# The second product of the last 768 tokens by seven block products in place of eight

## The chip, the cores and the metric

The kernel runs on one core of a Trainium2 chip. The metric is device microseconds of one execution, the median of several. PE is the engine that multiplies matrices, PEld its weight loads, DVE the vector engine, ACT the scalar engine, SP the queue from which all transfers (DMAs) of this kernel are issued.

## The reference, cut to what matters

Three stages follow each other on 4 x 576 = 2304 tokens of width 512: attention, a gated block (`_moe_ref`), and this block, the only one that the change touches:

```python
def _moe2_ref(x, g_ln, w_ch1, w_ch2) -> np.ndarray:    # x 2304 x 512, w_ch1 512 x 2048, w_ch2 2048 x 512
    mu = np.mean(x, axis=-1, keepdims=True)
    var = np.mean((x - mu) ** 2, axis=-1, keepdims=True)
    xn = (x - mu) / np.sqrt(var + 1e-06) * g_ln
    ch = np.maximum(xn @ w_ch1, 0.0) @ w_ch2
    return (x + ch).astype(np.float32)
```

Everything is float32. The kernel splits each operand into a high and a low part (`split`: ACT writes the high part, DVE the difference) and adds three matmuls for one product: low weight by high data, high by low, high by high.

## The kernel before

The last stage, `last_stage`, does `_moe2_ref` in three thirds of 768 tokens (`sc` = 0, 1, 2; `TC`, `TH` = 768, 384), each third in two halves of 384. Features lie on the 128 partitions, tokens along the row.

**First product.** The 2048 hidden features are 16 blocks of 128, worked in 8 pairs. `pair` does a pair for both halves at once: a 2 x 2 block product (2 halves by 2 feature blocks) by seven block products with sums of weights and of data (Strassen's scheme in Winograd's form) in place of eight. One `product` is 6 matmuls of 128x384, a pair 42. The combined weights `w1[i]` of a pair are made in the first third (`piece`, `combine`), written to HBM (`keep`) and read back in the other thirds (`fetch`, 1792 KB) into two buffers in turn: the fetch for pair i + 2 can start when pair i has done its last matmul. The sums of the seven products go through DVE: u2 = p6 + p1, u3 = p7 + u2, and so on (lines 839 to 865); p1 is copied by ACT (`s`, L840), since p2 is added onto it in its bank.

**Second product.** It is done straight (`ch2`): for a hidden block f, 4 output blocks of 128 features, 3 matmuls each, 12 in all. Half 0 runs among the pairs, two pairs' blocks behind; the hidden blocks of half 1 are kept unsplit (`late`) and half 1 follows after the pairs, each block split by `to_h` (L793 on ACT, L794 on DVE) three buffers ahead of PE. A third is 336 matmuls of the first product and 384 of the second. `leave` scales each output block by the row's factor, adds x and stores it (L826, L828, L829).

**Beside it.** `prepare` works through `units`: loading and converting the weights in the first third (DVE, ACT). `norm`, `expand` and `rsqrt` make the next third's normalised data, on DVE and ACT. The program is written in this order, but a planner, with costs of its own, sets the order on every engine: it may move an instruction ahead of one that it takes to be waiting. On the chip each engine then runs its own list in order, and a waiting instruction holds back all behind it; that goes for SP's list of transfers too.

## Time and profile before

| | us |
|---|---|
| median of 3 runs (lowest, highest) | 687.57 (685.63, 692.07) |
| the profiled execution | 686.18 |
| its span, first to last instruction | 684.4 |
| first matmul of the last stage's first product | 296.5 |
| last matmul of the kernel starts | 679.83 |

The profile page gives busy time and instructions of each engine, the chain that ended last, and groups of equal instructions with their mean time. A matmul's bar lasts some 335 ns while the next starts some 174 ns after it, since they are pipelined: PE's rate is to be read from starts, not from bars. The granted clock is full throughout (0.999 in the mean). The views used further on are shown as rows ahead of the prediction.

### The profile page before, as it was taken

How to read it: one execution, taken by the hardware profiler on the slowest of the kernel's cores; microseconds unless marked ns; L12 is line 12 of the kernel's file. 1: busy time of each engine (PE TensorE's matmuls, PEld its weight loads, DVE VectorE, ACT ScalarE, POOL GpSimd, SP SyncE). 2: the span in 40 equal slices, each digit the busy share in tenths (PEclk: the TensorE clock that was granted, in tenths of full speed). 3: DMA queues.
4: the chain of work that ended last, by engine and by line, in shares of the span. 5: the costliest groups of instructions: out<-in, count | busy, mean ns of one | idle time of the engine just before them, and what ended most of it. 6: DMA issues, size and time to landing. Idle time of an engine off the chain costs nothing.

```text
span 684.4 us, 12749 instructions
## 1 busy us (share of the span) xinstructions
PE 663.7 (97%) x5050; PEld 635.6 (93%) x5050; DVE 466.2 (68%) x990; ACT 318.9 (47%) x794; POOL 19.6 (3%) x24
## 2 busy tenths in 40 slices
PE   5899999999998999999999999999999999999997
PEld 4689979989897989989999999999999999999997
DVE  4989787586759686899989993733669355333523
ACT  3988966283458447644454952111365222111121
POOL 0011011000200011000000000000000000000000
PEclk9999999999999999999999999999999999999999
DMA  8873233457552550449796634534354425352001
GB/s 267 290 195 121 85 100 114 141 157 213 161 149 78 167 181 1 169 165 387 253 347 232 247 132 160 196 136 191 124 199 154 139 75 210 121 203 107 25 23 46
DMA packets 34987, 110.58 MB, mean 162 GB/s; under 512 B 3760, under 2 KB 14256, under 8 KB 31856
## 3 DMA queue, kind: packets, MB, share of 16 engines
q1 hardware_dynamic: 34928, 109.78, 47.1%
q8 instruction: 39, 0.64, 0.4%
q14 instruction: 20, 0.16, 0.1%
HBM read 83.02 MB, written 26.74 MB: 160 GB/s over the span
## 4 chain that ended last, share of the span: by engine, by line
PE 69%; DVE 10%; DMA 8%; ACT 8%; issue 2%; SPq 1%; POOL 1%; DVEq 0%; ACTq 0%; POOLq 0%
PE ps_p L788 24%; PE ps_o L204 10%; PE ps_o L205 10%; PE ps_o L203 9%; DMA w_scratch<-w_p 3%; ACT pt L400 2%; DMA qk<-in_qk_l 2%; PE ps_g L203 1%; PE ps_pv L458 1%; DMA y_scratch<-y 1%; PE ps_g L205 1%; DMA n<-y_scratch 1%; PE ps_g L204 1%; PE ps_t L439 1%; ACT pts L400 1%
## 5 line engine op out<-in xcount | busy, mean ns | idle before, releaser
L788 PE MATMUL ps_p<-x,w 128*128 128x384 f32 x1008 | 184.1, 335 | 1.3 <-DVE u L844 1.1
L788 PEld LDWEIGHTS ps_p<-x,w 128*128 128x128 f32 x1008 | 175.0, 188 | 3.0 <-DVE u L844 1.5
L205 PE MATMUL ps_o<-h,w 128*128 128x384 f32 x384 | 128.3, 334 | 0.0
L204 PE MATMUL ps_o<-h,w 128*128 128x384 f32 x384 | 128.3, 334 | 0.0
L203 PE MATMUL ps_o<-h,w 128*128 128x384 f32 x384 | 126.8, 334 | 0.1
L203 PEld LDWEIGHTS ps_o<-h,w 128*128 128x128 f32 x384 | 71.9, 188 | 0.4 <-ACT h L793 0.4
L204 PEld LDWEIGHTS ps_o<-h,w 128*128 128x128 f32 x384 | 72.1, 188 | 0.1
L205 PEld LDWEIGHTS ps_o<-h,w 128*128 128x128 f32 x384 | 72.1, 188 | 0.0
L794 DVE SCALAR_TENSOR_TENSOR h<-late,h 128x384 fp32r<-128x384 f32 x48 | 26.5, 556 | 41.6 <-ACT h L793 41.6
L793 ACT ACTIVATE h<-late 128x384 fp32r<-128x384 f32 x48 | 25.3, 526 | 63.4 <-PE ps_o L205 63.2
L840 ACT ACTIVATE s<-ps_p 128x384 f32<-128x384 f32 x24 | 11.8, 491 | 58.9 <-PE ps_p L788 56.1
L203 PE MATMUL ps_g<-wsg,vn 128*128 128x288 f32 x128 | 39.0, 304 | 0.0
L205 PE MATMUL ps_g<-wsg,vn 128*128 128x288 f32 x128 | 38.2, 299 | 0.0
L203 PE MATMUL ps_u<-xhl,winl 128*128 128x288 f32 x128 | 38.1, 297 | 0.0
L793 ACT ACTIVATE h<-c 128x384 fp32r<-128x384 f32 x24 | 12.6, 524 | 54.3 <-DVE c L857 54.2
L204 PE MATMUL ps_g<-wsg,vn 128*128 128x288 f32 x128 | 37.9, 296 | 0.0
L203 PE MATMUL ps_y<-gt,wout 128*128 128x288 f32 x128 | 37.8, 298 | 0.0
L204 PE MATMUL ps_u<-xhl,winh 128*128 128x288 f32 x128 | 37.8, 295 | 0.0
L205 PE MATMUL ps_u<-xhl,winh 128*128 128x288 f32 x128 | 37.7, 295 | 0.0
L205 PE MATMUL ps_y<-gt,wout 128*128 128x288 f32 x128 | 37.5, 295 | 0.0
L204 PE MATMUL ps_y<-gt,wout 128*128 128x288 f32 x128 | 37.5, 294 | 0.0
L203 PE MATMUL ps_v<-winh,xhl 128*128 128x512 f32 x80 | 31.9, 399 | 0.3 <-DVE xhl L495 0.2
(179 smaller groups left out, 1316.4 us busy)
## 6 DMA issues: line engine op xcount, KB each, us to landing
w<-w_scratch SPq DMA_DIRECT2D x16, 1792.0 KB, 7.5
w_scratch<-w SPq DMA_DIRECT2D x8, 1792.0 KB, 7.5
stg<-in_w_ch SPq DMA_DIRECT2D x22, 512.0 KB, 6.2
raw_p<-in_w_ch SPq DMA_DIRECT2D x20, 256.0 KB, 3.1
qk<-in_qk_s SPq DMA_DIRECT2D x8, 601.0 KB, 4.5
...
```

The costliest lines, as they stand in the source:

```text
L203: nc.tensor.matmul(ps, lhsT=ll, rhs=rh, start=first, stop=False)
L204: nc.tensor.matmul(ps, lhsT=lh, rhs=rl, start=False, stop=False)
L205: last_mm[0] = nc.tensor.matmul(ps, lhsT=lh, rhs=rh, start=False, stop=last)
L400: exps.append(nc.scalar.activation(p3[:, i, :], src, AF.Exp, scale=SCALE, bias=mx[:, i:i + 1], accum_out=sm[:, i:i + 1]))
L439: nc.tensor.transpose(ps[:rows, (t - t0) * c:(t - t0 + 1) * c], src, ident)
L458: nc.tensor.matmul(ps[64 * h:64 * h + 64, (i - b0) * QB:(i - b0 + 1) * QB], lhsT=vt[:LW, (i * 2 + h) * D:(i * 2 + h + 1) * D], rhs=pT[:LW, ...
L788: nc.tensor.matmul(o, lhsT=w[:, a, n0 + nk * k, :], rhs=x[:, c, k, :], start=first and k == 0 and n == 0, stop=k == 1 and n == 2, skip_gro ...
L793: nc.scalar.activation(h[:, 0, :], src, AF.Relu)
L794: nc.vector.scalar_tensor_tensor(out=h[:, 1, :], in0=src, scalar=0.0, in1=h[:, 0, :], op0=ALU.max, op1=ALU.subtract)
L840: nc.scalar.activation(s1, a, AF.Copy)
```

## The change

The second product of the last third is done by seven block products too, over 2 halves by 2 sets of output blocks, with the sum over the 8 pairs accumulated in PSUM. The last third so becomes two stretches: `last_pair` eight times (336 matmuls, no second product among them), and then seven products of 48 matmuls (336). The operands:

- The weights of the second product are combined too. `store2` writes each pair's converted weights to HBM in the first third (512 KB); `combine2` in the second third reads them back, makes four sums on DVE, splits 1792 columns (ACT, DVE) and stores high and low parts as 14 pieces of 128 columns a partition (runs of 512 bytes; a partition's 14 pieces lie 1 MiB apart in `w2_scratch`), 896 KB each. `fetch2` reads one slice of 1024 KB for each product and output set in the last third, into four buffers in turn.
- The hidden blocks stay in SBUF as sums (`hb`) and are split for the next product by `grain` while PE does the present one.
- `out2` adds up the products and stores the outputs.

In the other two thirds `pair` gets another order, in which p6, p5 and p3 are added onto p1's bank and p4 onto p7's (the sign of one data sum is turned for it). DVE makes two sums fewer a pair; ACT makes copies of the running sum (`u2`, `u4`) and one relu more. The steps of `norm` in the first third stand earlier.

```diff
+WX2 = {1: (0, 2, 0), 2: (4, 2, 2), 7: (1, 2, 1), 4: (5, 2, 2), 5: (8, 1, 0), 6: (10, 1, 1), 3: (12, 1, 3)}
+ORDER2 = (1, 2, 7, 6, 5, 4, 3)
+XTAGS = (0, 4, 1, 5, 2, 3, 6)
...
-NORM_AT = ({3: (0,), 4.5: (1,), 5: (2,), 5.5: (3,), 6: (4,), 6.5: (5,)}, {2: (0,), 3: (1,), 4: (2,), 5: (3,), 6: (4,), 6.5: (5,)})
+NORM_AT = ({1: (0,), 3: (1,), 3.5: (2,), 4.5: (3,), 5: (4,), 6: (5,)}, {2: (0,), 3: (1,), 4: (2,), 5: (3,), 6: (4,), 6.5: (5,)})
...
+    w2f_d = nc.dram_tensor("w2f_scratch", (NW, P, 2 * DM), F32, kind="Internal").ap()
+    w2_d = nc.dram_tensor("w2_scratch", (14, P, NW, 2, P), F32, kind="Internal").ap()
...
+    def store2(i):
+        nc.sync.dma_start(out=w2f_d[i], in_=big["stg"][:, 2048:3072].bitcast(F32))
+
+    def combine2(i):
+        stg = big["stg"]
+        c = stg[:, 0:1792].bitcast(F32)
+        wf = c[:, 0:1024].rearrange("p (k e r f) -> p k e r f", k=2, e=2, r=2)
+        nc.sync.dma_start(out=c[:, 0:1024], in_=w2f_d[i])
+        s = c[:, 1024:1792].rearrange("p (s e f) -> p s e f", s=3, e=2)
+        a11, a21, a12, a22 = wf[:, 0, :, 0], wf[:, 0, :, 1], wf[:, 1, :, 0], wf[:, 1, :, 1]
+        tt = nc.vector.tensor_tensor
+        tt(out=s[:, 0], in0=a21, in1=a22, op=ALU.add)
+        tt(out=s[:, 1], in0=s[:, 0], in1=a11, op=ALU.subtract)
+        tt(out=a21, in0=a11, in1=a21, op=ALU.subtract)
+        tt(out=s[:, 2], in0=a12, in1=s[:, 1], op=ALU.subtract)
+        hi, lo = stg[:, 1792:3584].bitcast(F32R), stg[:, 0:1792].bitcast(F32R)
+        split(hi, lo, c)
+        for h, src in enumerate((hi, lo)):
+            nc.sync.dma_start(out=w2_d[:, :, i, h, :].rearrange("n p f -> p n f"),
+                              in_=src.bitcast(F32).rearrange("p (n f) -> p n f", f=P))
+
+    w2s, slices = {}, {}
+    places = (("w2", 0), ("w2", NW - 1), ("w1", 0), ("w1", 1))
+
+    def fetch2(n):
+        m, e = ORDER2[n // 2], n % 2
+        n0, step, _ = WX2[m]
+        place = places[n % 4]
+        shape = [P, 2, 2, DM] if place[0] == "w2" else [P, 2, 14, P]
+        w = big[place].tile(shape, F32R, tag=place[0], name="w2c")
+        w = w.rearrange("p a b c -> p (a b c)")[:, :2 * NW * P]
+        nc.sync.dma_start(out=w.bitcast(F32), in_=w2_d[n0 + step * e].rearrange("p i h f -> p (i h f)"))
+        slices[m, e] = w.rearrange("p (i h f) -> p i h f", i=NW, h=2)
...
+        units += [(store2, (i,))]
...
-                tt(out=b21, in0=t2, in1=b21, op=ALU.subtract)
+                tt(out=b21, in0=b21, in1=t2, op=ALU.subtract)
...
-        b = bank(role, "ps_p6")[:, :TH]
-        product(sc, i, b, 6, True)
+        b = bank(role, "ps_p7")[:, :TH]
+        product(sc, i, b, 7, True)
+        product(sc, i, a, 6, False)
         u2 = tmp("u2")
-        tt(out=u2, in0=b, in1=s1, op=ALU.add)
-        product(sc, i, a, 2, False)
-        h1 = to_h(a)
-        d = bank(role, "ps_p7")[:, :TH]
-        product(sc, i, d, 7, True)
-        u3 = tmp("u3")
-        tt(out=u3, in0=d, in1=u2, op=ALU.add)
+        nc.scalar.activation(u2, a, AF.Copy)
+        c = bank(role, "ps_p2")[:, :TH]
+        product(sc, i, c, 2, True)
+        c11 = tmp("c11")
+        tt(out=c11, in0=c, in1=s1, op=ALU.add)
+        h1 = to_h(c11)
+        product(sc, i, a, 5, False)
+        u4 = tmp("u4")
+        nc.scalar.activation(u4, a, AF.Copy)
+        tt(out=late(f2), in0=b, in1=u4, op=ALU.add)
         if i:
             ch2(sc, 0, f1 - 2, 1 - role)
         mid()
-        e = bank(role, "ps_p4")[:, :TH]
-        product(sc, i, e, 4, True)
+        product(sc, i, a, 3, False)
+        nc.scalar.activation(late(f1), a, AF.Relu)
+        product(sc, i, b, 4, False)
         c21 = tmp("c21")
-        tt(out=c21, in0=u3, in1=e, op=ALU.subtract)
+        tt(out=c21, in0=b, in1=u2, op=ALU.add)
         h2 = to_h(c21)
-        c = bank(role, "ps_p5")[:, :TH]
-        product(sc, i, c, 5, True)
-        tt(out=late(f2), in0=c, in1=u3, op=ALU.add)
         if i:
             ch2(sc, 0, f2 - 2, 1 - role)
-        product(sc, i, c, 3, False)
-        tt(out=late(f1), in0=c, in1=u2, op=ALU.add)
...
+                        prepare(len(units[done[0]:]) if i + 3 == NW else 7)
                         if i < NW - 2:
                             keep(i + 2)
-                elif i + 2 < NW:
-                    fetch(i + 2)
+                else:
+                    if i + 2 < NW:
+                        fetch(i + 2)
+                    combine2(i)
...
+        last_chunk(NSC - 1)
...
+    def last_pair(sc, i, b):
+        tt = nc.vector.tensor_tensor
+        relu = lambda dst, src: nc.scalar.activation(dst, src, AF.Relu)
+        a = bank8("ps_p1")[:, :TH]
+        product(sc, i, a, 1, True)
+        s1 = tmp("s1")
+        nc.scalar.activation(s1, a, AF.Copy)
+        o = bank8("ps_p6")[:, :TH]
+        product(sc, i, o, 6, True)
+        u2 = tmp("u2")
+        tt(out=u2, in0=o, in1=s1, op=ALU.add)
+        product(sc, i, a, 2, False)
+        relu(b[:, 0], a)
+        d = bank8("ps_p7")[:, :TH]
+        product(sc, i, d, 7, True)
+        u3 = tmp("u4")
+        tt(out=u3, in0=d, in1=u2, op=ALU.add)
+        c = bank8("ps_p5")[:, :TH]
+        product(sc, i, c, 5, True)
+        tt(out=b[:, 3], in0=c, in1=u3, op=ALU.add)
+        relu(b[:, 3], b[:, 3])
+        e = bank8("ps_p4")[:, :TH]
+        product(sc, i, e, 4, True)
+        tt(out=b[:, 2], in0=u3, in1=e, op=ALU.add)
+        relu(b[:, 2], b[:, 2])
+        product(sc, i, c, 3, False)
+        tt(out=b[:, 1], in0=c, in1=u2, op=ALU.add)
+        relu(b[:, 1], b[:, 1])
...
+    def grain(m, g):
+        b = hb[g]
+        tt = nc.vector.tensor_tensor
+        if m == 6:
+            tt(out=b[:, :, 1], in0=b[:, :, 3], in1=b[:, :, 0], op=ALU.subtract)
+        elif m == 4:
+            tt(out=b[:, :, 2], in0=b[:, :, 1], in1=b[:, :, 2], op=ALU.subtract)
+        j = XTAGS[grain_turn[0] % 7]
+        grain_turn[0] += 1
+        x = big["x", 0 if j in (0, 4) else 1].tile([P, 2, 2, TH], F32R, tag=f"x{j}", name=f"t{j}")
+        split(x[:, :, 0], x[:, :, 1], b[:, :, WX2[m][2]])
+        for i in range(2):
+            grans[m, 2 * g + i] = x[:, i]
...
+    def last_chunk(sc):
+        tt = nc.vector.tensor_tensor
+        first_a = big["nm"].tile([P, NLATE, TH], F32R, tag="n0", name="t_a")
+        first_b = big["lt"].tile([P, NF - NLATE, TH], F32R, tag="lt", name="t_b")
+        for i in range(NW):
+            g = i // 2
...
+            b = hb[g][:, i % 2]
+            last_pair(sc, i, b)
+            x = first_a[:, 2 * i:2 * i + 2] if 2 * i < NLATE else first_b[:, 2 * i - NLATE:2 * i - NLATE + 2]
+            split(x[:, 0], x[:, 1], b[:, 0])
+            grans[1, i] = x
+            if i % 2:
+                b2 = hb[g]
+                tt(out=b2[:, :, 0], in0=b2[:, :, 1], in1=b2[:, :, 0], op=ALU.subtract)
+                tt(out=b2[:, :, 1], in0=b2[:, :, 3], in1=b2[:, :, 1], op=ALU.subtract)
+            if i + 2 < NW:
+                fetch(i + 2)
+            if i in (1, 3):
+                fetch2(i // 2)
+            if i == NW - 3:
+                residual(sc, 0)
+            if i >= NW - 2:
+                rsqrt(sc, i + 2 - NW)
+        pair_tile = lambda: big["h"].tile([P, 2, TH], F32R, tag="h", name="pt").bitcast(F32)
+        ps, s1, u2, u3 = {}, pair_tile(), pair_tile(), pair_tile()
+        for n, m in enumerate(ORDER2):
+            if n + 1 < len(ORDER2):
+                for e in range(2):
+                    fetch2(2 * n + 2 + e)
+                for g in range(NW // 2):
+                    grain(ORDER2[n + 1], g)
+            onto = {2: 1, 3: 5}.get(m)
+            for e in range(2):
+                ps[m, e] = ps[onto, e] if onto else bank8("ps_c")[:, :TH]
+            order = [(i, e) for i in range(NW) for e in range(2)]
+            if n + 1 == len(ORDER2):
+                order.sort(key=lambda ie: ie[1])
+            for i, e in order:
+                w, x = slices[m, e], grans[m, i]
+                for k, (a, c) in enumerate(((1, 0), (0, 1), (0, 0))):
+                    nc.tensor.matmul(ps[m, e], lhsT=w[:, i, a, :], rhs=x[:, c, :], start=not onto and i == 0 and k == 0,
+                                     stop=i == NW - 1 and k == 2, skip_group_check=True)
+                if i == NW - 1:
+                    out2(sc, m, e, ps[m, e], s1[:, e], u2[:, e], u3[:, e])
...
+        if m == 1:
+            nc.scalar.activation(s1, o, AF.Copy)
+        elif m == 2:
+            finish(0, 0, o)
+        elif m == 7:
+            p7[e] = o
+        elif m == 6:
+            tt(out=u2, in0=o, in1=s1, op=ALU.add)
+            tt(out=u3, in0=p7[e], in1=u2, op=ALU.add)
+        elif m == 5:
+            t = tmp("u2")
+            tt(out=t, in0=o, in1=u3, op=ALU.add)
+            finish(1, 1, t)
+        elif m == 4:
+            t = tmp("u2")
+            tt(out=t, in0=u3, in1=o, op=ALU.subtract)
+            finish(0, 1, t)
+            y = ys[sc, 1, 2 * e]
+            tt(out=u2, in0=u2, in1=rbs[sc][:, 1, :], op=ALU.mult)
+            tt(out=y, in0=u2, in1=y, op=ALU.add)
+        else:
+            finish(1, 0, o)
...
-    prepare(max(0, 13 - done[0]))
+    prepare(max(0, 14 - done[0]))```

PE, the last third. Before, pair 2 (w_0_6723 is its weight buffer; a pair's second product lies between its first-product parts):

```order
L788 MATMUL ps_p_6814<-x_6188,w_0_6723 128x384 x6
L788 MATMUL ps_p_6823<-x_6216,w_0_6723 128x384 x6
L788 MATMUL ps_p_6814<-x_6249,w_0_6723 128x384 x6
L788 MATMUL ps_p_6841<-x_6291,w_0_6723 128x384 x6
L203 MATMUL ps_o<-h,w_3_4404 128x384
...
L788 MATMUL ps_p_6862<-x_6309,w_0_6723 128x384 x6
L788 MATMUL ps_p_6874<-x_6342,w_0_6723 128x384 x6
...
L788 MATMUL ps_p_6874<-x_6192,w_0_6723 128x384 x6
```

Now, the same pair (w_0_6611), and then the start of the seven products (ps_c, from the slices w2c):

```order
L833 MATMUL ps_p_6682<-x_6256,w_0_6611 128x384 x6
L833 MATMUL ps_p_6691<-x_6284,w_0_6611 128x384 x6
L833 MATMUL ps_p_6682<-x_6317,w_0_6611 128x384 x6
L833 MATMUL ps_p_6707<-x_6359,w_0_6611 128x384 x6
L833 MATMUL ps_p_6716<-x_6410,w_0_6611 128x384 x6
L833 MATMUL ps_p_6725<-x_6377,w_0_6611 128x384 x6
L833 MATMUL ps_p_6716<-x_6260,w_0_6611 128x384 x6
L833 MATMUL ps_p_6746<-x_6256,w_1_6677 128x384 x6
...
L1052 MATMUL ps_c<-t_a,w2c 128x384 x30
L1052 MATMUL ps_c<-t_b,w2c 128x384 x18
L1052 MATMUL ps_c<-t_7103,w2c 128x384 x12
```

The 24 matmuls of the second product inside a pair are gone; the pairs stand back to back.

SP, the end of the pairs of the second third. Before, the two weight fetches for the last third (w_0, w_1) and the first stores of outputs:

```order
L653 DMA w_1_5894<-w_scratch 128x3584
L653 DMA w_0_6181<-w_scratch 128x3584
L653 DMA w_1_6183<-w_scratch 128x3584
L829 DMA out<-yr 128x384 x2
L821 DMA yr<-y_scratch 128x384 x2
```

Now (L677 is the load of `combine2`, L688 its stores, L658 a weight fetch):

```order
L658 DMA w_1_5935<-w_scratch 128x3584
L677 DMA stg<-w2f_scratch 128x1024
L658 DMA w_0_6249<-w_scratch 128x3584
L688 DMA w_scratch<-stg 128x14x128 x2
L658 DMA w_1_6251<-w_scratch 128x3584
L677 DMA stg<-w2f_scratch 128x1024
L874 DMA out<-yr 128x384 x2
```

Loads and stores of `combine2` stand among the fetches; the last of them is issued right behind the fetch of w_1.

DVE, the same place: the first outputs of half 0 leave (`o<-ps_o,rb`), and hidden blocks of half 1 are split (`h<-late`). Before:

```order
L794 SCALAR_TENSOR_TENSOR h<-late,h 128x384
L826 TENSOR_TENSOR o<-ps_o,rb 128x384 x2
L828 TENSOR_TENSOR yr<-o,yr 128x384 x2
L826 TENSOR_TENSOR o<-ps_o,rb 128x384 x2
L794 SCALAR_TENSOR_TENSOR h<-late,h 128x384
```

Now:

```order
L839 SCALAR_TENSOR_TENSOR h<-late,h 128x384
L871 TENSOR_TENSOR o<-ps_o,rb 128x384 x2
L681 TENSOR_TENSOR stg<-stg 128x256
L873 TENSOR_TENSOR yr<-o,yr 128x384
L682 TENSOR_TENSOR stg<-stg 128x256
L683 TENSOR_TENSOR stg<-stg 128x2x128
L684 TENSOR_TENSOR stg<-stg 128x256
L873 TENSOR_TENSOR yr<-o,yr 128x384
L871 TENSOR_TENSOR o<-ps_o,rb 128x384 x2
L839 SCALAR_TENSOR_TENSOR h<-late,h 128x384
L185 TENSOR_TENSOR stg<-stg 128x1792
```

The first sum of a `combine2` (L681), which needs the load on SP, stands between the leaving outputs and the fourth hidden block of half 1.

## Rows read from the trace of the kernel before

**Rows 1.** The page, part 1: busy time, share of the span, instructions.

```profile
span 684.4 us, 12749 instructions
PE 663.7 (97%) x5050; PEld 635.6 (93%) x5050; DVE 466.2 (68%) x990; ACT 318.9 (47%) x794; POOL 19.6 (3%) x24
```

**Rows 2.** Busy time by stretch: stretch, length, PE, PEld, DVE, ACT, POOL; clock; DMA share.

```profile
330.00:350.00 20.00, 20.00 (x118) 20.00 (x117) 18.76 (x33) 9.90 (x13) 0.00 (x0) 1.00 0.91 342
...
500.00:520.00 20.00, 20.00 (x118) 20.00 (x117) 14.96 (x28) 11.89 (x22) 0.00 (x0) 1.00 0.33 106
520.00:540.00 20.00, 20.00 (x117) 20.00 (x116) 15.41 (x28) 7.25 (x13) 0.00 (x0) 1.00 0.64 233
...
620.00:640.00 20.00, 20.00 (x118) 20.00 (x117) 6.75 (x13) 3.02 (x6) 0.00 (x0) 1.00 0.26 93
```

**Rows 3.** Waits: engine and line, waited for; us in total, times, longest.

```profile
PE ps_p L788 <- DVE u L844: 1.1, 1, 1.1
...
PE ps_p L788 <- DVE h L794: 0.2, 1, 0.2
```

**Rows 4.** Groups of instructions on PE: count, busy us, mean ns.

```profile
L788 PE MATMUL ps_p<-x,w 128*128 128x384 f32 x1008 | 184.1, 335 | 1.3 <-DVE u L844 1.1
```

**Rows 5.** Timeline of PE, last third: start, length, merged count.

```profile
555.15 11.13 PE L788 MATMUL ps_p<-x,w 128*128 128x384 f32 x63
```

**Rows 6.** Timeline, the end of the kernel.

```profile
679.83 0.34 PE L205 MATMUL ps_o<-h,w 128*128 128x384 f32 x1
680.27 0.55 DVE L826 TENSOR_TENSOR o<-ps_o,rb 128x384 f32<-128x384 f32 x1
680.85 0.56 DVE L828 TENSOR_TENSOR yc<-o,yc 128x384 f32<-128x384 f32 x1
```

**Rows 7.** Transfers, 470 to 525 us, then 570 to 640: count, KB, landing us.

```profile
w<-w_scratch SPq DMA_DIRECT2D x5, 1792.0 KB, 7.1
...
w<-w_scratch SPq DMA_DIRECT2D x5, 1792.0 KB, 7.7
...
DMA to landing us min/median/max: 7.0/7.7/8.7
```

**Rows 8.** Timeline, end of pair 1 of the last third.

```profile
572.88 1.72 PE L788 MATMUL ps_p<-x,w 128*128 128x384 f32 x9
574.11 0.33 SPq L653 DMA_DIRECT2D w<-w_scratch  x1
```

**Rows 9.** DMA queue in 20:40, 600:640, 640:684: packets, MB, share of 16 engines.

```profile
q1 hardware_dynamic: 3065, 5.28, 90.1%
...
q1 hardware_dynamic: 397, 5.00, 33.0%
...
q1 hardware_dynamic: 1152, 1.57, 10.0%
```

**Rows 10.** Groups of instructions on DVE and ACT, 440 to 684 us.

```profile
L865 DVE TENSOR_TENSOR late<-ps_p,u 128x384 f32<-128x384 f32 x15 | 8.4, 557 | 24.4 <-PE ps_p L788 24.4
...
L840 ACT ACTIVATE s<-ps_p 128x384 f32<-128x384 f32 x14 | 6.9, 492 | 45.6 <-PE ps_p L788 45.6
L180 DVE TENSOR_TENSOR x<-yc,x 128x768 fp32r<-128x768 f32 x7 | 6.6, 953 | 0.0
```

**Rows 11.** Timeline, first third: the split of 1792 columns on ACT and DVE.

```profile
311.18 1.71 ACT L179 ACTIVATE w<-stg 128x1792 fp32r<-128x1792 f32 x1 [1.35 <-PE ps_p L788]
...
312.92 2.03 DVE L180 TENSOR_TENSOR w<-stg,w 128x1792 fp32r<-128x1792 f32 x1 [0.72 <-ACT w L179]
```

**Rows 12.** Timeline, second third: last weight fetch, first outputs of half 0.

```profile
517.90 0.32 SPq L653 DMA_DIRECT2D w<-w_scratch  x1
...
524.01 1.02 DVE L826 TENSOR_TENSOR o<-ps_o,rb 128x384 f32<-128x384 f32 x2
```

**Rows 13.** Landing of 512 KB loads (L188), then 256 KB (L628), 296 to 384.

```profile
DMA to landing us min/median/max: 3.2/7.3/10.2
...
DMA to landing us min/median/max: 2.6/3.1/4.2
```

More of the change, by code (lines that the diff above doesn't have):

```diff
@@ L873, in last_stage @@
     def last_stage():
-        for sc in range(NSC):
+        for sc in range(NSC - 1):
             role = sc % 2
@@ L893, in last_stage @@
                 leave(sc, 0, d)
-            if sc + 1 < NSC:
-                fetch(0)
-                fetch(1)
+            fetch(0)
+            fetch(1)
             for f in range(NF):
                 hs[f] = to_h(late(f))
-                if sc + 1 < NSC and f in EXPAND_AT:
+                if f in EXPAND_AT:
                     expand(sc + 1, EXPAND_AT.index(f))
@@ new lines, in mixer_kernel, with out2, finish @@
+    p7 = {}
+    def out2(sc, m, e, o, s1, u2, u3):
+        tt = nc.vector.tensor_tensor
+        def finish(half, r, src):
+            y = ys.pop((sc, half, 2 * e + r))
+            t = big["tmp"].tile([P, TH], F32, tag="o", name="o", bufs=2)
+            tt(out=t, in0=src, in1=rbs[sc][:, half, :], op=ALU.mult)
+            tt(out=y, in0=t, in1=y, op=ALU.add)
+            cs = slice(sc * TC + half * TH, sc * TC + (half + 1) * TH)
+            nc.sync.dma_start(out=out[2 * e + r, :, cs], in_=y)
+        if m == 1:
[18 more added lines that the diff above has]
+            tt(out=y, in0=u2, in1=y, op=ALU.add)
+        else:
+            finish(1, 0, o)
@@ L962, in open_c @@
         right(("x", 1))
-        right(("w2", 1))
-        right(("w2", 2))
+        right(("w2p", 0))
     def open_d():
         close("dn", "dw", "cw")
-        for i in range(3, NW):
-            right(("w2", i))
+        for i in (1, 2):
+            right(("w2p", i))
+        right(("w2", NW - 1))
         right("h", 3)
@@ L975, in open_d @@
         big["late", 0] = big["nm"].tile([P, NLATE, TH], F32, tag="n0", name="late")
-        big["late", 1] = big["lt"].tile([P, NF - NLATE, TH], F32, name="late2")
+        big["late", 1] = big["lt"].tile([P, NF - NLATE, TH], F32, tag="lt", name="late2")
     last = B - 1
```

28 lines of the change are left out of this document (20 added, 8 removed).

## The prediction

> **What bounds the kernel now.** I read the page's list of engines first: PE is busy 97% of the span, DVE 68% [rows 1]. Then the windows over the last stage: PE is busy in all of each stretch at clock 1.00, and in the first third DVE (18.76 of 20 us) and the transfers (share 0.91) are nearly full as well [rows 2]. The list of waits shows PE stopped in its products for only 1.1 and 0.2 us [rows 3]. So the last stage is as long as PE's row of matmuls. What one costs is not its bar of 335 ns [rows 4], but the interval of starts: 63 matmuls of which the last lasts 0.33 us take 11.13 us, so (11.13 − 0.33)/62 = 0.1742 us [rows 5]. Behind the last matmul come two DVE operations and a store [rows 6]; the changed kernel ends in the same way, so the tail is worth nothing.
>
> The sum is made against the profiled execution, 686.18 us, which is 1.39 below the median of three (687.57).
>
> **The parts.**
>
> a) Removed: the last third has 336 + 336 matmuls in place of 336 + 384. 48 × 0.1742 = **−8.36**, all on the path.
>
> b) The pairs of the last third lose their cover. A pair was 42 + 24 = 66 matmuls, 11.5 us; now it is 42 × 0.1742 = 7.31. The 1792 KB fetch of pair i + 2 waits for pair i's last matmul and has pair i + 1's time to land. In the same third it landed in 7.0 to 8.7 us, median 7.7; in the second third the median was 7.1 [rows 7]. It was issued 0.19 behind the pair's end: the sixth matmul's slot ends at 572.88 + 6 × 0.1742 = 573.92, the issue stands at 574.11 [rows 8]. That makes 7.89 against 7.31, or 6.79 for pair 1, from which the order hoists three matmuls. With two buffers a late fetch gives its successor more time, so stalls come at every second pair: 1.10 + 0.58 + 0.58 = 2.3. By 7.1 it would be 0.5, by 8.7 it would be 5.3. I take **+2.3** (0.5 to 5.3), since 7.7 was measured in this very stretch.
>
> The Trainium skill, "DMA: Bandwidth & Descriptors", section on the anatomy of one DMA, fits 2.0 us plus bytes by 436 GB/s: 6.2 us for 1792 KB. By that the fetch would fit into a pair, this term would be 0 and the sum about 681. The measured landings disagree; the fit was made on GpSimd's queue, here SP issues.
>
> c) The seven products (48 matmuls, 8.36 us) fetch two 1024 KB slices each, a product ahead. 600 to 640 us moved 5.00 MB in 0.330 × 40 × 16 = 211 engine-us [rows 9], that is 379 GB/s from 16 engines: 2.77 us a slice, 4.84 for 1792 KB, which leaves 7.7 − 4.84 = 2.86 of fixed time. Both have landed after 0.19 + 2.86 + 5.54 = 8.6; the second is wanted three matmuls into the next product, 8.9. Just in time: **+0.3** (0 to 1.5).
>
> d) Product 2 is added onto product 1's bank, so PE waits there for ACT's copy, 0.49 us [rows 10], less the three matmuls of the other bank: **+0.2**.
>
> e) The pairs' sums now come without matmuls of the second product between them. A DVE sum of 0.557 or an ACT copy of 0.492 [rows 10] has one product (6 × 0.174 = 1.05 us) as its cover, enough unless DVE or ACT is late with a split or with `rsqrt`: **+0.5** (0 to 1.5). The splits for the seven products cost DVE 0.953 each [rows 10], four in 8.36 us: hidden.
>
> f) `combine2` in the second third: four short sums, a split of 1792 columns (ACT 1.71, DVE 2.03 for the same in the first third [rows 11]), a load and two stores, each beside PE. DVE has room: 14.96 and 15.41 of 20 us before [rows 2], and the pairs give two sums back. But one L681 stands in DVE's list between the first outputs of half 0 and the fourth hidden block of half 1, and its load is queued on SP right behind a 1792 KB fetch. Before, that fetch was issued at 517.90 and the first outputs left at 524.01, 6.1 behind it [rows 12]. A 512 KB load landed in 3.2 to 10.2 us (median 7.3) where transfers queued, a 256 KB one in 2.6 to 4.2 [rows 13]. Behind 4.84 us of another transfer it lands some 8 to 9.3 us after that issue, so DVE stands still from about 7.2 for 0.8 to 2.1 us; the fourth block's low part comes late and PE stands for about as long: **+1.3** (0 to 3.5).
>
> g) The first third. `store2` adds 512 KB a pair, 1.38 us at 379 GB/s; transfers of 0.91 × 11.5 = 10.5 us a pair become 11.9 against PE's 11.5. DVE, the other engine near its limit there, gives back two sums a pair (1.1 us); the one long wait of 1.1 may go, since its sum does. Were all six loaded pairs held up by 0.4 the price would be 2.4, with ACT's new copies on the path up to 6: **+1.0** (−1.1 to 6).
>
> Sum: −8.36 + 2.3 + 0.3 + 0.2 + 0.5 + 1.3 + 1.0 = −2.8, so 683.4 against 686.18. The median of three may again lie up to 1.4 above one execution; I add half: **684.1**. All terms at their low ends give 686.18 − 8.4 − 0.4 = 677.4, all at their high ends 686.18 − 8.4 + 18 = 696.
>
> **The rivals.**
>
> *Nothing stalls* (chance 0.20). Fetches land in about 7.0 as the quickest did [rows 7], L681's load arrives before DVE reaches it, and the first third stays bound by PE: terms b to g together at most 1.5, so 677.8 to 679.3. For it: PE hardly waits anywhere now, and DVE gets lighter. Against: in the stretch at issue the median was 7.7, over the 7.31 of a pair.
>
> *Slower: the stores of `combine2` hold up SP* (0.12). They write runs of 512 bytes. No row shows such a store; the nearest are the last stretch, 0.10 × 44 × 16 = 70 engine-us for 1152 packets, 61 ns each of 1.4 KB, and 20 to 40 us with 288 engine-us for 3065 packets, 94 ns each of 1.7 KB [rows 9]. Less the bytes at 23.7 GB/s an engine that is 3.6 to 21 ns a packet; with 22 ns for 512 bytes it makes 25 to 43 ns, 112 packets an engine, 2.8 to 4.8 us a store. The next load writes over what the stores read, so a chain is load (3.1 to 7.3), four short sums and the splits of [rows 11] (together about 5.5), and two stores with 0.9 on top for the fixed part beyond what they overlap (6.5 to 10.5). By the order the eight begin some 18 us ahead of the second third and end some 15 us into the last; with a third of 720 × 0.1742 = 125 us that is 158/8 = 19.7 us for each, and a chain takes 15 to 23. With a short load it decides from (19.7 − 3.1 − 5.5 − 0.9)/2 = 5.1 us a store: at 8 us a chain lasts 25.5 and eight of them are 46 us late; the fetches queued on SP behind their loads come late with them, PE waits, about 725. A little over 5 costs 4 to 8: 688 to 691. Against it: it takes packets dearer than both rows have them, or long loads every time, and the DMA engines were busy for only 0.33 and 0.64 of the time there [rows 2].
>
> The Trainium skill, "DMA: Bandwidth & Descriptors", section on latency and other measured facts, speaks against this change: rows of a tensor in HBM lying large powers of two apart are slow (207 GB/s at a pitch of 512 KiB, 164 at 2 MiB). A partition's pieces lie 1 MiB apart here, though the partitions themselves only 8 KB; by those figures a store would take an estimated 4.4 to 5.6 us, which is this rival's milder form. No run here shows such a pitch.
>
> *The first third becomes bound by transfers or by ACT* (0.15): term g at 4 to 6, the rest as above, so 687 to 689. For it: the share of 0.91 and DVE at 94% [rows 2], and ACT gets a copy between two products on one bank, behind splits of 1.71. Against: ACT is busy only 9.9 of 20 us there, and transfers run ahead of their use.
>
> *My forecast* (0.53): the row of PE shortens, and half to three quarters is given back in stalls at fetches and one at L681; 681 to 687.
>
> **How the numbers follow.** A measurement of this kernel can tell about 1%, 6.9 us, from no change. Faster by that means under 680.7: the first rival, 0.20. Within 1% lie the forecast, nearly all of the third rival and the milder end of the second, 0.64. Slower means over 694.4: the dear form of the second, and forecasts and third rivals with several terms at their high ends at once, 0.16. The range leaves out the dear form above and the last us of full gain below: 677.5 to 693.
>
> **What the profile will show.** Right: 48 matmuls fewer on PE; the product's matmuls of the last third waiting for a transfer of w at pairs 3, 5 and 7 for 0.5 to 1.1 us each; one wait of the second product at the start of half 1 of the second third, with DVE held at L681. Wrong: landings of 1792 KB under 7.1 between the pairs (then b goes and the first rival holds); stores of `combine2` landing over 8 us with SP's issues late at the start of the last third (second rival); waits on ACT's u2 or on pieces of weights in the first third over 3 us (third). A wait of PE in the seven products over 1.5 us would show c wrong, and a chain that ends elsewhere than with PE would overturn the whole sum.

## The result, and the profile after

The changed kernel takes 695.24 us (median of 4 runs, 693.15 to 697.56) against 687.34 before: 1.0105 times as long, with an interval of 1.0075 to 1.0135. The prediction was 684.1, its range 677.5 to 693.0: the time is 2.2 us above the range, and the change costs about 8 us where some 3 were to be gained. The prediction had given a time over 694.4 a chance of 0.16.

The profiled execution has 693.15 us. The page, its engines, answering to [rows 1]:

```profile
span 691.0 us, 12856 instructions
PE 660.8 (96%) x5002; PEld 626.8 (91%) x5002; DVE 507.7 (73%) x1026; ACT 376.1 (54%) x884; POOL 19.8 (3%) x24
```

The 48 matmuls are gone (5002 for 5050). PE is busy for only 2.9 us less, and the span is 6.6 longer. The list of PE's waits in the last stage (what PE worked on, the operation waited for, us in total, times, longest), answering to [rows 3]:

```profile
PE ps_p L833 <- DVE w L185: 3.6, 1, 3.6
PE ps_p L833 <- ACT u L898: 2.4, 2, 1.8
PE ps_p L833 <- DMA w<-w_scratch: 1.2, 2, 0.8
PE ps_c L1052 <- DMA w2c<-w_scratch: 1.0, 1, 1.0
PE ps_p L833 <- DVE c L894: 0.7, 1, 0.7
PE ps_o L208 <- ACT h L838: 0.4, 1, 0.4
PE ps_p L833 <- ACT s L885: 0.3, 1, 0.3
```

Before there were 1.3 us of such waits. The greatest is new: the pair waits for its split weights. It stands at the end of the first third, where nothing was removed. Timeline of PE, with the idle time ahead in brackets, and DVE's operation that ended it:

```profile
384.47 0.34 PE L210 MATMUL ps_o<-h,w2p 128*128 128x384 f32 x1
388.42 3.01 PE L833 MATMUL ps_p<-x,w 128*128 128x384 f32 x12 [3.61 <-DVE w L185]
391.75 4.14 PE L833 MATMUL ps_p<-x,w 128*128 128x384 f32 x18 [0.33 <-ACT s L885]
```

```profile
386.33 2.03 DVE L185 TENSOR_TENSOR w<-stg,w 128x1792 fp32r<-128x1792 f32 x1
```

Windows there (columns as in [rows 2]):

```profile
384.00:388.00 4.00, 0.81 (x5) 0.48 (x3) 3.70 (x6) 3.81 (x6) 0.00 (x0) 1.00 0.90 344
388.00:390.00 2.00, 1.58 (x9) 1.59 (x10) 2.00 (x5) 0.00 (x0) 0.00 (x0) 0.98 1.11 430
390.00:392.00 2.00, 1.68 (x6) 1.17 (x5) 1.93 (x5) 1.73 (x3) 0.00 (x0) 0.50 0.94 394
392.00:394.00 2.00, 2.00 (x9) 2.00 (x10) 2.00 (x3) 1.55 (x4) 0.00 (x0) 0.67 0.99 423
```

PE stands for 3.6 us, and just after that the granted clock is 0.50 (1.2 GHz) from 390 to 392 and 0.67 in the mean of the next two: 15 matmuls in four us, where [rows 5] have 23. Busy time hides losses of two kinds: a slow matmul is busy for longer, and one that starts up to 0.16 us late leaves no gap between bars of some 335 ns. So PE's busy time fell by 2.9 us and not by 8.4, and waits and busy time alone don't add up here.

A better account takes the start of every matmul. Between the first matmul of a third's first product and that of the next third, PE's time beyond its number of matmuls times 0.1734 us (the commonest interval) is what that stretch loses. I call it "over the row". The last stretch ends with the kernel's last matmul. The first matmul's own shift stands beside it.

| | stage starts | first third | second | last |
|---|---|---|---|---|
| before | 296.55 | 2.0 | 0.0 | 0.0 |
| changed | 297.22 | 8.6 | 3.2 | 4.6 |

0.7 + 6.6 + 3.2 + 4.6 − 48 × 0.1734 = +6.8, and the span says +6.6. The 0.7 is left without a cause: over all kernels below the stage starts between 296.5 and 301.1, whatever was changed. All that follows is told in this measure, one profiled execution of each kernel.

### The profile page after: what moved, and what is told of

Read it like the earlier page. It is cut to its first block, busy times and chain, and to the rows that moved or that the text cites. A ratio compares the mean times of both kernels' runs of the same rounds, so it can differ in the third digit from the quotient of the medians.

```text
span 691.0 us, 12856 instructions
## 1 busy us (share of the span) xinstructions
PE 660.8 (96%) x5002; PEld 626.8 (91%) x5002; DVE 507.7 (73%) x1026; ACT 376.1 (54%) x884; POOL 19.8 (3%) x24
## 4 chain that ended last, share of the span: by engine, by line
PE 55%; DVE 15%; DMA 13%; ACT 11%; issue 3%; POOL 1%; SPq 1%; DVEq 0%; ACTq 0%; POOLq 0%
PE ps_p L833 19%; PE ps_c L1052 7%; PE ps_o L208 4%; PE ps_o L209 4%; PE ps_o L210 4%; DMA w<-w_scratch 2%; DMA w_scratch<-w_p 2%; ACT pt L405 2%; DMA qk<-in_qk_l 2%; DMA w_scratch<-stg 2%; DMA stg<-in_w_ch 2%; PE ps_y L208 2%; PE ps_y L210 1%; PE ps_y L209 1%; PE ps_t L444 1%
## 5 line engine op out<-in xcount | busy, mean ns | idle before, releaser
L833 PE MATMUL ps_p<-x,w 128*128 128x384 f32 x1008 | 187.8, 339 | 8.3 <-DVE w L185 3.6
L833 PEld LDWEIGHTS ps_p<-x,w 128*128 128x128 f32 x1008 | 175.1, 189 | 14.8 <-DVE w L185 3.9
L209 PE MATMUL ps_o<-h,w2p 128*128 128x384 f32 x192 | 64.3, 335 | 0.0
L210 PE MATMUL ps_o<-h,w2p 128*128 128x384 f32 x192 | 64.2, 334 | 0.0
L208 PE MATMUL ps_o<-h,w2p 128*128 128x384 f32 x192 | 62.3, 335 | 0.4 <-ACT h L838 0.4
L1052 PE MATMUL ps_c<-t,w2c 128*128 128x384 f32 x288 | 50.5, 335 | 1.1 <-DMA w2c<-w_scratch 1.0
L1052 PEld LDWEIGHTS ps_c<-t,w2c 128*128 128x128 f32 x288 | 49.9, 188 | 1.7 <-DMA w2c<-w_scratch 1.3
L208 PE MATMUL ps_g<-wsg,vn 128*128 128x288 f32 x128 | 39.0, 305 | 0.0
L210 PE MATMUL ps_g<-wsg,vn 128*128 128x288 f32 x128 | 38.2, 299 | 0.0
L208 PE MATMUL ps_u<-xhl,winl 128*128 128x288 f32 x128 | 38.1, 297 | 0.0
L208 PE MATMUL ps_y<-gt,wout 128*128 128x288 f32 x128 | 37.9, 298 | 0.1
L210 PE MATMUL ps_u<-xhl,winh 128*128 128x288 f32 x128 | 37.7, 295 | 0.0
L210 PE MATMUL ps_y<-gt,wout 128*128 128x288 f32 x128 | 37.5, 295 | 0.0
L208 PEld LDWEIGHTS ps_o<-h,w2p 128*128 128x128 f32 x192 | 35.8, 188 | 0.7 <-ACT h L838 0.7
L209 PEld LDWEIGHTS ps_o<-h,w2p 128*128 128x128 f32 x192 | 36.0, 188 | 0.4 <-DVE h L839 0.2
L210 PEld LDWEIGHTS ps_o<-h,w2p 128*128 128x128 f32 x192 | 36.1, 188 | 0.0
L838 ACT ACTIVATE h<-late 128x384 fp32r<-128x384 f32 x32 | 16.7, 524 | 35.1 <-PE ps_o L210 30.5
L184 ACT ACTIVATE t<-hb 128x768 fp32r<-128x768 f32 x24 | 20.2, 846 | 23.5 <-PE ps_c L1052 23.0
L208 PE MATMUL ps_v<-winh,xhl 128*128 128x512 f32 x80 | 31.9, 399 | 0.3 <-DVE xhl L500 0.2
## 6 DMA issues: line engine op xcount, KB each, us to landing
w<-w_scratch SPq DMA_DIRECT2D x16, 1792.0 KB, 7.7
w_scratch<-w SPq DMA_DIRECT2D x8, 1792.0 KB, 7.6
```

Source lines behind the costliest of these rows:

```text
L184: nc.scalar.activation(dst_h, src, AF.Copy)
L208: nc.tensor.matmul(ps, lhsT=ll, rhs=rh, start=first, stop=False)
L209: nc.tensor.matmul(ps, lhsT=lh, rhs=rl, start=False, stop=False)
L210: last_mm[0] = nc.tensor.matmul(ps, lhsT=lh, rhs=rh, start=False, stop=last)
L833: nc.tensor.matmul(o, lhsT=w[:, a, n0 + nk * k, :], rhs=x[:, c, k, :], start=first and k == 0 and n == 0, stop=k == 1 and n == 2, skip_gro ...
L838: nc.scalar.activation(h[:, 0, :], src, AF.Relu)
```

## Experiments

Ratios are to the kernel before in the same job (687.3 to 688.3 us); where two kernels of different jobs are compared, the ratios are the fairer measure. "Last split" is when DVE begins the last split of 1792 columns for the pairs (line 185; 180 or 186 in some kernels), counted from the stage's start.

| kernel | median us | ratio (interval) | first, second, last third over the row | last split |
|---|---|---|---|---|
| changed | 695.24 | 1.0105 (1.0075, 1.0135) | 8.6, 3.2, 4.6 | 89.1 |
| no_store2 | 692.43 | 1.0059 (1.0040, 1.0078) | 4.0, 1.0, 10.6 | 84.9 |
| yc_early | 695.93 | 1.0114 (1.0089, 1.0138) | 9.2, 3.2, 5.2 | 89.2 |
| own_w2 | 697.61 | 1.0146 (1.0116, 1.0177) | 3.9, 9.0, 8.1 | 85.5 |
| pair_only | 694.34 | 1.0090 (1.0069, 1.0111) | 8.4, 0.4, 0.2 | 85.4 |
| pair_norm | 689.55 | 1.0030 (1.0003, 1.0057) | 2.2, 0.5, 0.2 | 83.5 |
| old_pair | 704.70 | 1.0249 (1.0209, 1.0288) | 11.7, 2.8, 12.3 | 89.7 |
| old_pair_own | 704.26 | 1.0232 (1.0202, 1.0262) | 3.9, 14.4, 8.8 | 85.1 |
| fetch_half | 698.40 | 1.0150 (1.0122, 1.0178) | 8.4, 3.9, 7.0 | 89.1 |
| store2_alone | 695.79 | 1.0105 (1.0053, 1.0157) | 9.6, 0.4, 0.2 | 89.7 |
| prep_only | 697.67 | 1.0131 (1.0077, 1.0184) | 7.5, 4.6, 0.6 | 88.4 |
| own_fine | 695.15 | 1.0094 (1.0062, 1.0127) | 4.5, 5.1, 7.9 | 85.6 |
| own_fine_pool | 706.65 | 1.0265 (1.0207, 1.0322) | 3.5, 11.3, 12.3 | 84.8 |
| after_yr | 715.88 | 1.0396 (1.0352, 1.0439) | 8.8, 13.2, 18.3 | 89.3 |
| own_fine_yr | 712.07 | 1.0329 (1.0279, 1.0380) | 3.3, 11.1, 19.1 | 84.4 |
| w2_pad | 697.94 | 1.0131 (1.0095, 1.0167) | 8.6, 5.3, 5.8 | 89.2 |

**What makes the last weights late.** The first four.

```diff
 # no_store2
     def store2(i):
-        nc.sync.dma_start(out=w2f_d[i], in_=big["stg"][:, 2048:3072].bitcast(F32))
+        pass
-        nc.sync.dma_start(out=c[:, 0:1024], in_=w2f_d[i])
+        nc.sync.dma_start(out=c[:, 0:1024], in_=w1_d[i][:, 0:1024])
```

> The changed kernel without store2's transfers (8 x 512 KB in the first third); combine2 loads 512 KB of the first product's weights instead, so the last third's second product is not the reference's. The planner then puts the 1536 KB load of yc ahead again, where it stood before. Theory A (the transfers of the first third: yc's load and store2 in front of the loads of raw weights make one cycle of the weights' chain 6 us longer, the last pair's weights come 6.7 us late, PE waits 3.6 us and then runs at half clock for 3.4 us): 6 to 7 us less than the changed kernel, about 688.5, no wait of PE on a split of w, clock 1.00 throughout. Theory C (the new order of the pairs, ACT's copies and DVE's list, delays the conversions): no difference, 693 to 697, the wait stays.

The wait on the split is gone and the first third gives back 4.6, with the clock at 1.00 there: the late weights are theory A's, not C's. But the time fell by only some 3, not to theory A's 688.5. The planner's lists had moved, and the last third now loses 10.6: PE waits 1.9 us for outputs that leave on DVE (L871), the clock is 0.5 for 3.4 us from 565.7, and 1.7 follow on a sum (L979).

```diff
 # yc_early
-NORM_AT = ({1: (0,), 3: (1,), ...
+NORM_AT = ({-0.5: (0,), 3: (1,), ...
```

> The changed kernel with one number altered: the step of norm that loads yc (1536 KB) in the first third is put half a pair into pair 0, so that on SP it stands one pair and a half earlier, as before the change; store2 stays. Theory A1 (it is the place of yc's load that counts): 5 to 7 us less, 688 to 690, the last pair's weights split by about 382. Theory A2 (store2's own 512 KB a pair, 1.4 us of transfers in each of eight cycles, is enough): at most 2 us less. Theory C: no difference.

A1 fell: the last split is as late as ever. The splits of w follow each other by 13.7, 16.1, 11.5, 13.4, 12.4 and 19.3 us here, by 13.7, 11.9, 11.5, 17.6, 12.3 and 19.3 in the changed kernel. The load of yc lengthens the cycle whose raw loads stand behind it, wherever that is, and the sum stays. In no_store2, where that load also stands early, they follow by 13.9, 13.9, 11.3, 11.2, 12.6 and 19.2. Against yc_early, with yc's load in the same place to within 2 us, the stores of store2 so cost 4.3 us.

```diff
 # own_w2 (store2 as in no_store2)
-        nc.sync.dma_start(out=c[:, 0:1024], in_=w2f_d[i])
+        nc.vector.tensor_tensor(out=c[:, 0:1024], in0=w2[i][:, 0] ..., in1=w2[i][:, 1] ..., op=ALU.add)
```

> The changed kernel in which combine2 makes its operand by adding the high and low parts of w2 that lie in SBUF anyway (one DVE sum of 1024 columns, about 1.2 us), so that store2 and combine2's load are not needed: 8 MB less of transfers. Theory A: first third as without store2, 6 to 7 us less; and if DVE's wait at L681 for its load caused the 1.8 us wait at 451 us, that goes too: 686 to 687.5, level with the kernel before. Theory C: 693 or more, since DVE has more to do.

The first third is as without store2. The time is not: the second third loses 9.0. The new sum of 1024 columns waits up to 2.4 us on DVE for the stores of the `combine2` before it, and PE then waits 2.1 us for ACT's copy (`u`), which stands behind the split on ACT; half clock follows another wait (538.4, 3.4 us). That 697.6 lies where theory C had put it is luck: theory C is about the first third, which is not slow here.

```diff
 # pair_only: the kernel before with
+ pair() of the changed kernel, the sign of t4 turned for it, and one buffer for u2 in place of two
```

> The kernel before with only the new order of the pairs (p6, p5, p3 added onto p1's bank, p4 onto p7's, ACT's copies) in all three thirds, and nothing else of the change. Theory A: within 1.5 us of the kernel before (687.3), PE waits under 2 us more in sum. Theory C: 3 to 6 us slower, with waits of PE on ACT's u and on splits of w late in the first third.

Theory C seemed to be shown by this: 6.4 us from the pairs' order alone, all in the first third. But here the waits are others, for hidden blocks (h, 2.1 and 1.9 us in four waits) and not for w; the two longest lie at 398 to 406, where `norm` and `expand` crowd ACT.

**Pairs, store2 and combine2 one by one.** Next came this kernel with the second half of that edit.

```diff
 # pair_norm: pair_only with
-NORM_AT = ({3: (0,), 4.5: (1,), 5: (2,), 5.5: (3,), 6: (4,), 6.5: (5,)}, ...
+NORM_AT = ({1: (0,), 3: (1,), 3.5: (2,), 4.5: (3,), 5: (4,), 6: (5,)}, ...
```

> The kernel before with the new order of the pairs in all three thirds and with the new places of norm's steps in the first third; no store2, no combine2, no seven products at the end. Alone, the pairs' order had cost 6.4 us, nearly all in the first third (PE's time over its row of matmuls there 8.4 us against 2.0 before), with the last of norm's products on PE at 396.3 against 389.7. Theory C1 (the new pairs make norm late, and only that): with the earlier steps it is gone, within 1.5 us of the kernel before. Theory C2 (ACT's copies and DVE's order slow the first third whatever norm does): still 3 us or more slower than before. If the changed kernel's first third (8.6 over the row) is the pairs plus store2, this kernel's should be like that without store2, about 4.

Nearer to C1: with `norm` earlier, the new pairs cost 0.3 us in the first third and 2 us in all, at the edge of what can be told from nothing and a little over C1's 1.5. The first third was not "about 4" either: 2.2. So the new pairs need `norm`'s new places, and the two together are no main cost. To this kernel I added the rest piece by piece.

```diff
 # store2_alone: pair_norm with (and the buffers of w2 laid out as in the changed kernel)
+        units += [(store2, (i,))]
-                        prepare(... else 6)
+                        prepare(... else 7)
```

> The kernel with the pairs' new order and norm's new places (689.6 us measured, PE 2.2 us over its row in the first third, the last split of w 83.6 us into the stage) with one thing added: store2, 8 x 512 KB in the first third, which nothing reads; all three thirds as before. Theory A2 (store2's transfers lie in the cycle load, convert, combine, split of each pair's weights, and that is why PE waits): the last split of w comes 4 to 6 us later (88 to 90 us into the stage), PE waits 2 to 5 us for it and the clock falls: 5 to 7 us more than without, 694 to 697. Theory E (it is combine2's first load and DVE sums at the end of the third, not store2): no more than 1.5 us over 689.6.

A2 is shown: store2 alone, whose data nothing reads, costs 5 to 6 us (5.2 by the ratios, whose intervals just touch, 6.2 by the medians 689.55 and 695.79). The profiled executions show where: 7.4 more in the first third. Its own wait on PE:

```profile
391.02 5.49 PE L833 MATMUL ps_p<-x,w 128*128 128x384 f32 x16 [3.58 <-DVE w L185]
```

Windows of pair_norm, then of store2_alone, at the cycle of the weights that becomes longer and at the wait:

```profile
340.00:352.00 12.00, 12.00 (x70) 11.68 (x69) 10.19 (x17) 6.82 (x11) 0.00 (x0) 1.00 0.84 305
...
383.00:395.00 12.00, 11.73 (x67) 11.09 (x66) 10.85 (x20) 10.62 (x18) 0.00 (x0) 1.00 0.72 270
```

```profile
340.00:352.00 12.00, 12.00 (x71) 11.91 (x70) 9.84 (x17) 5.12 (x11) 0.00 (x0) 1.00 0.98 389
...
383.00:395.00 12.00, 8.01 (x34) 7.25 (x33) 11.43 (x21) 9.61 (x15) 0.00 (x0) 0.77 0.90 340
```

With store2 the transfers are full (0.98, 389 GB/s) while DVE and ACT are less busy. SP in store2_alone, and the first conversion of the loads that it issues (L193):

```profile
331.13 0.42 SPq L654 DMA_DIRECT2D w_scratch<-w  x1
331.59 0.44 SPq L768 DMA_DIRECT2D yc<-y_scratch  x1
334.59 0.32 SPq L671 DMA_DIRECT2D w2f_scratch<-stg  x1
335.02 2.24 SPq L193 DMA_DIRECT2D stg<-in_w_ch  x2
```

```profile
348.04 0.66 ACT L197 ACTIVATE stg<-stg 128x512 f32<-128x512 f32 x1
```

1792, 1536 and 512 KB stand in front of the raw weights; by 379 GB/s that is 10.4 us. The conversion begins 13.0 after the issue, and most of that is the landing of the two raw loads, in store2_alone and then in pair_norm:

```profile
DMA to landing us min/median/max: 11.2/11.2/11.3
```

```profile
DMA to landing us min/median/max: 7.5/7.7/7.8
```

The split that ends this cycle is 17.6 us behind the one before it, 10.9 in pair_norm. Of these, 7.9 and 2.5 us lie ahead of the landing of the second raw load, 9.7 and 8.4 behind it: 5.3 us of the difference are late data, and 1.3 are DVE's and ACT's lists, in which operations on yc now stand. The store's reading of the staging buffer held nothing up here, since it landed at 344.94, ahead of the first raw load (346.18). PE needs a pair's weights every 11.5 to 13 us here, so the 6 us are never made good. Over all kernels: the eight with store2 have the last split at 88.4 to 89.7 us into the stage, the nine without it (the kernel before among them) at 83.1 to 85.6, whatever their lists. store2 also brings another place for yc's load, but that place by itself changes nothing (yc_early), and with the load in the same cycle store2 still costs 4.3 (yc_early against no_store2).

```diff
 # prep_only: store2_alone with
+                    if sc == 1:
+                        combine2(i)
```

> The same with combine2 in the second third as well; the last third still by pairs and eight products, so that what combine2 writes is not read. By the changed kernel's trace: 2 to 3 us more than with store2 alone in the second third (a wait of PE behind a split of 1792 columns on ACT, and short ones), 697 to 700. If the second third shows under 1 us over PE's row, the changed kernel's 3.2 there came from its list of instructions and not from combine2.

The time is as expected (1.9 us more, inside the intervals), and the second third rises by more: 4.6, of which some 1.7 are half clock for 3.4 us from 452.0. Steps of one piece each so give: pairs and `norm` 0.3 in the first third; store2 7.4 there; `combine2` 4.2 in the second third; the new last third 4.0 of its own against 8.3 saved. These are not sizes that add up exactly. The first third falls by 2.2 from store2_alone to prep_only, which do the same in it (half clock for 6.8 us in one and 3.4 in the other), and in the changed kernel the second third is 1.4 lower than in prep_only: after the same wait its clock stayed full.

How `combine2` does it, read in the changed kernel (DVE, ACT, PE):

```profile
447.43 0.42 DVE L681 TENSOR_TENSOR stg<-stg 128x256 f32<-128x256 f32 x1 [2.31 <-DMA stg<-w2f_scratch]
```

```profile
450.42 1.70 ACT L184 ACTIVATE stg<-stg 128x1792 fp32r<-128x1792 f32 x1 [2.88 <-DVE stg L684]
```

```profile
452.96 1.32 PE L833 MATMUL ps_p<-x,w 128*128 128x384 f32 x6 [1.84 <-ACT u L898]
```

DVE stands 2.3 us for the load, the split on ACT begins just before a pair needs ACT's copy of its running sum, and the copy stands behind its 1.70 us. That the load is to blame for where the split falls is read from this one place and not tested: own_w2 has no such load and loses 9.0 in this third.

**The last third, and a better version.**

```diff
 # fetch_half: in the last third
-        nc.sync.dma_start(out=w ..., in_=w1_d[i])
+        nc.sync.dma_start(out=w ...[:, :14 * P], in_=w1_d[i][:, :14 * P])
-                nc.tensor.matmul(o, lhsT=w[:, a, ...
+                nc.tensor.matmul(o, lhsT=w[:, 0, ...
```

> The changed kernel, but in the last third the first product uses the high part of the weights only (in all three of its matmuls), so that its fetches are 896 KB in place of 1792; all instructions on PE, DVE and ACT stay. The output is not the reference's. By term b of the prediction the stalls between the pairs (2.8 us of PE's time in the trace) go: the pairs' waits for a transfer of w under 0.2 us, and 2 to 3 us less than the changed kernel, unless the planner's lists move.

Half right. From the fourth pair on, the pairs start 7.3 to 7.4 us apart (7.4 to 7.9 in the changed kernel), so full fetches do cost stalls between the pairs. But a wait of 2.9 us ends at 585.61, for a fetch that SP issued at 578.14, right behind loads of x for the outputs, and half clock follows. The expected fall of 2 to 3 us came out as a rise of 3.

```diff
 # old_pair: the changed kernel with pair() and NORM_AT of the kernel before
 # old_pair_own: that, and own_w2's edits
```

> The changed kernel with the pairs of the first two thirds, and norm's steps, as they were before the change; store2, combine2 and the new last third stay. Theory C (the pairs' order is a main cost): 3 to 6 us less than the changed kernel, 689 to 692. Theory A2 (store2's transfers make the weights' chain late whatever the pairs do): the wait on the last split of w stays, and the time with it, 694 to 697.

> The pairs and norm as before the change, and combine2 adds up the parts of w2 in SBUF, so that there is neither store2 nor combine2's load; the new last third stays. If pairs, store2 and loads are the costs, the first third is back at 2 us over PE's row, the second at 1 to 3 (DVE has 1.2 us more for each combine2), the last at 4 to 5: 688.0 - 8.4 + 5 = 684 to 686, faster than both. Theory D (each new list of the planner costs 3 to 8 us somewhere, whatever is taken out): 690 or more, with the waits in other places.

Both are worse (704.7, 704.3): old_pair lies above both of its forecasts, old_pair_own where theory D has it. With the old pairs, two sums a pair more on DVE, the wait on the split of w is 5.2 us in place of 3.6, so it is not the new order that brings it; old_pair loses 12.3 in the last third besides. Theory D holds as far as this goes: old_pair_own has its first third at 3.9, and loses 14.4 in the second, 7.8 of them in one wait for a split of data on ACT.

```diff
 # own_fine: own_w2 with (and its sum of 1024 columns in two of 512)
-        split(hi, lo, c)
+        for k in range(4):
+            cs = slice(448 * k, 448 * k + 448)
+            split(hi[:, cs], lo[:, cs], c[:, cs])
 # own_fine_pool: that, with fetch (last third) and fetch2 on nc.gpsimd
 # after_yr, own_fine_yr: the changed kernel, own_fine, with yr's loads and the stores in leave on nc.gpsimd
```

> Neither store2 nor combine2's load (the parts of w2 in SBUF are added), and combine2's work in short pieces: two sums of 512 columns, four splits of 448. With one split of 1792 columns this kernel took 697.6 us, with 9 us over PE's row in the second third and 8 in the last. If the long operations in front of the pairs' short ones are what costs there, the second third falls to 2 to 4 and the time to 690 to 693. If it is the places of the operations in the lists, it stays within 2 us of 697.6.

> As the one with short pieces, and the last third's fetches of w and of slices are issued by GpSimd, which has nothing else to do there, in place of SP, where a fetch stood behind loads and stores of outputs (issued 3 us after its buffer was free in the version with one split, PE waited 3.2 us, then ran at half clock). If SP's line is the cause, the last third falls from 8 to 3 or 4 us over PE's row, in all 686 to 689; if the fetches' own landing time is, no change in the last third.

> The changed kernel with the loads of x for the outputs (yr) and the stores of the outputs of the first two thirds issued by GpSimd, which has nothing else to do there, in place of SP. Theory S (part of the 4.6 us that the last third lies over PE's row comes from SP's line: the fetch for pair 2 of the last third stands behind yr's loads, which wait for outputs to be stored): the fetch is issued within 0.3 us of its pair's end, the last third falls to 2.5 to 3.5 us, the time by 1 to 2 us. Theory T (it is the fetches' landing time against a pair of 7.3 us): the last third stays at 4 to 5.

> The kernel without store2 and with combine2 in short pieces (695.2 us; 4.5, 5.1 and 7.9 us over PE's row in the three thirds; in the last PE waits 3.2 us for a fetch that SP issues late, and then runs at half clock), with yr's loads and the outputs' stores of the first two thirds issued by GpSimd. Theory S: the last third falls to 3 to 4, the time to 690 to 691. Theory T: 694 to 697 as before.

Short pieces bring the second third from 9.0 to 5.1, less than expected (2 to 4; some 1.7 of the 9.0 were half clock); in all 695.15, where 690 to 693 had been expected, since the last third keeps its 7.9. All three attempts to relieve SP's line made it much worse, and neither theory S nor T has it. own_fine_pool loses 11.3 already in the second third, ahead of the fetches that it moves. In after_yr the fetches' waits on PE went from 1.2 to 0.3 us, but not by theory S: in the changed kernel each fetch between the pairs was already issued within 0.02 us of the end of the matmul that it waited for (at 574.06 for pair 2). It is in fetch_half, own_w2 and own_fine that this fetch stands right behind yr's loads. What after_yr lost came on DVE:

```profile
452.97 0.56 DVE L873 TENSOR_TENSOR yr<-o,yr 128x384 f32<-128x384 f32 x1 [9.99 <-DMA yr<-y_scratch]
```

DVE holds its line for 10 us for a load of 192 KB whose buffer had first to be stored. GpSimd issued it at 444.79, 5.5 us behind that store, and it landed 8.1 us later. In the changed kernel SP issued the same load 5.0 us behind the store and it landed in 4.5, so most of the difference is the landing; its cause is open. PE waits 9.1 for a pair's operation behind it, and 8.3 more in the last third, where DVE stands 9.0 for another such load. The version that would beat both kernels was not found; nothing here was faster than the kernel before.

```diff
 # w2_pad
-    w2_d = nc.dram_tensor("w2_scratch", (14, P, NW, 2, P), ...
+    w2_d = nc.dram_tensor("w2_scratch", (14, P * NW * 2 * P + 1024), ...
+    w2_d = w2_d[:, :P * NW * 2 * P].rearrange("n (p i h f) -> n p i h f", p=P, i=NW, h=2)
```

> The changed kernel with the 14 pieces of a partition in w2_scratch 1 MiB + 4 KB apart in place of 1 MiB, every instruction's place unchanged. In the changed kernel a store of combine2 landed in 6.3 us (median; 896 KB), the estimate from packet times had been 5.7 to 7.7 with the fixed part. If the pitch of 1 MiB slows the stores, they land in 5.3 or less and the first fetches of the last third come earlier; if it does not, 6.0 to 6.6 and the same time, 693 to 697.

Landings of the 896 KB stores, min, median and max: 4.7, 6.3 and 10.4 us in the changed kernel, and in this one:

```profile
DMA to landing us min/median/max: 4.7/6.0/10.1
```

No effect of the pitch shows: 6.0 lies in the 6.0 to 6.6 that had been set for none, and the time is, if anything, longer (697.94, 0.9 over its forecast). The Trainium skill, "DMA: Bandwidth & Descriptors", section on latency and other measured facts, tells of slow transfers at pitches of large powers of two between partitions; here the partitions lie 8 KB apart and only the pieces 1 MiB, and these runs show no effect of that.

## Why the prediction failed, point by point

- **a, removed matmuls**: −8.36; measured 48 fewer at 0.1734, −8.3. Right.
- **b, fetches in the last third**: +2.3. Right in mechanism: the first fetch was issued 0.20 us behind its pair's last matmul, as the sum has it, and the fetches landed in 7.7, 8.1, 7.6, 6.9, 7.2 and 7.2 us. PE lost 1.05 and 0.66 at the third and fifth pair, where 1.10 and 0.58 stood in the sum, and no more than 0.1 at the seventh: 1.7 in all.
- **c, slices**: +0.3 (0 to 1.5). One wait of 1.0 and about 1.3 lost: mis-sized, inside its bounds. **d**: +0.2; 0.33 where product 2 goes onto product 1's bank. **e**: +0.5; from 568 to 614 us PE lost 2.9, so that beside b's 1.7 some 1.2 are left, in steps of about 0.1 us.
- **f, `combine2`**: +1.3 (0 to 3.5) against 3.2, inside its bounds. DVE did stand at L681 for its load, but in another place: early among the pairs of the second third, not at the start of half 1, where nothing over 0.2 us was lost. And the long split on ACT in front of a pair's copy, put under the third rival's arguments, was what PE waited for.
- **g, the first third**: +1.0 (−1.1 to 6) against 6.6, outside its bounds. This is the step that failed. I had the volume (11.9 us of transfers against 11.5 a pair), but made it 0.4 a pair and hid it behind "transfers run ahead of their use". They don't: with one staging buffer each cycle of load, conversion, sums and split is a chain, a longer one is handed on to the end of the third (the last split comes at 89.1, without store2 at 83 to 86), and there PE stands 3.6 us at once. Nor is yc's load of 1536 KB in that volume: before, it stood at 308 us, ahead of the stretch (330 to 350) from which I read the share of 0.91. Where it stands does not matter (yc_early); it lengthens whichever cycle it meets (to 16.1 or 17.6 from some 11.5). And no term allowed for the clock after a wait of PE, here some 1.7 us.
- **The rivals**: the third (first third bound by transfers) was the right one, with 0.15 and 687 to 689; its sign, a wait on pieces of weights in the first third of over 3 us, came (3.61). But it was priced at 4 to 6 for a stretch that lost 6.6, and its 687 to 689 missed as well. The second (stores slow) did not come: 6.3 us to land, by the packets' price 5.7 to 7.7 with the fixed part. The forecast's sum stood on terms b to e, which were right to 1.3 us together (3.3 against 4.6). Of the 9.6 us between that sum (−2.8) and the account (+6.8), g makes 5.6, f 1.9, b to e 1.3 and the stage's later start 0.7. The rest of the miss is that the median lies 2.1 above the profiled execution, where 0.7 had been added.
